# Whole-width 32x32 transposes, weight conversion on three engines, the Fourier stage beside held-back MLP tiles, and chunk loads in one piece, in a DeltaNet + Fourier-mix + MLP kernel

## The chip, the core and the metric

One core of a Trainium2 chip runs the whole program. The metric is device time in microseconds (us) of one execution, lower is better. [...] Each engine executes its own instructions strictly in the order in which they stand, and waits on semaphores for the others.

## The reference

Two blocks, joined by a reshape. `B, H, S, D = 4, 8, 768, 48`, so `DM = H*D = 384`, and the MLP is 384 -> 1536 -> 384.

```python
def _attn_ref(q, k, v, beta):
    k_n = k / (np.linalg.norm(k, axis=-1, keepdims=True) + 1e-06)
    state = zeros((B, H, D, D))
    for t in range(S):
        y[:, :, t] = einsum('bhd,bhde->bhe', q[:, :, t], state)
        v_old = einsum('bhde,bhd->bhe', state, k_n[:, :, t])
        state = state + beta_t * einsum('bhd,bhe->bhde', k_n[:, :, t], v[:, :, t] - v_old)
    return y

def _moe_ref(x, w_ch1, w_ch2):                # x = y as (B, S, DM)
    u = x + real(fft(fft(x, axis=1), axis=2))
    un = (u - mean(u)) / sqrt(var(u) + 1e-06)  # over the last axis
    return u + maximum(un @ w_ch1, 0) @ w_ch2
```

The MLP weights arrive as 64-bit floats, seen by the kernel as pairs of 32-bit words, and are turned into 32-bit floats on the chip.

## The kernel before, in words

**Attention, in chunks of 64 time steps.** A *step* `m` of the main loop is one chunk of one batch (12 chunks a batch, 48 steps). `chain(m)` does it for all 8 heads: `pk` (matmul with the state), `R` (DVE), `pu` (matmul with `wt`, the inverse of a 64x64 triangular matrix per chunk and head), `U` (ACT), `pS` and the new state `st` (DVE), then the output `py`, which ACT writes into `x`. The next step needs the new state.

**Preparation.** Four chunks of a batch are a *quad* `Q` (12 of them), two quads a *group* `g` (6 of them, 8 steps each). `prepare(Q)` loads k and q, normalises k (`Ksq`, `nrm`, `kp`), transposes both on PE (`pt`, `KQT`), makes the products `pg`, and masks them: DVE multiplies `pg` by `bm` (mask times beta, made on POOL) into `A`, and by the causal mask into `LQ`. `invert(g)` inverts the triangular matrices of a group: four DVE transposes of 32 partitions each (`X<-A`), 30 pairs of `sub`/`X` instructions of DVE that invert the 32x32 diagonal blocks, six more transposes (`wt<-X`, `T1<-X`), two rounds of small matmuls `pj` with ACT copies between them (`js`, `wt`) for the off-diagonal blocks, and a POOL multiplication of `wt` by beta. `ahead(g)` is the two `prepare` and the `invert` of a group, and runs as a generator (`pre`) during the eight steps of the group before.

**After a batch.** `post(b)` is the side generator (`side`) during the steps of the next batch: the Fourier stage (sums and differences of `x` into `scr`, matmuls `pf` and `pb`, eight DVE additions of each `pb` into `x`, the row statistics), then the MLP in three groups of 256 rows (`un`, `ptr`, `unT`; 12 tiles `ph`, each turned to `hT` by ACT and DVE in turn; `po`; the addition into `x`; the store). During batch 0 the side generator is `weights()`: six pieces of 1.5 MB land in the buffer that `hT` also uses, and each is converted in three parts of 512 columns, by ten DVE instructions and one POOL multiplication. After the last step, `post(3)` runs alone.

**Order.** In the main loop each step yields three times; between the yields the loop advances `pre` and `side` by fixed shares (6 and 8 a step). From the emitted program a scheduler makes each engine's instruction order; on the chip that order is fixed. The k, q and v chunks are loaded by SP, one DMA of 64 rows and four heads each (three DMAs at the middle of a sequence, where a row is skipped); k lands in `K4`, q in the only `qp` buffer.

Of the kernel before, what the change touches and what calls it, by code (L numbers as in the profile page):

```python
# [80 lines left out]
def kernel(  # L81
# [63 lines left out]
    def chunk_at(n):  # L145


        lo = n < NCH // 2
        return n * CH + (1 if lo else 0), CH - 1 if n == NCH // 2 - 1 else CH

    def fetch(Q, *pairs):
# [1 line left out]
        for dst, src in pairs:
            for hh in range(2):
                hs = slice(4 * hh, 4 * hh + 4)
                for c in range(QT):
                    t0, m = chunk_at(QT * i + c)
                    cuts = (0, m) if m == CH else (0, 48, m)
                    for a, z in zip(cuts, cuts[1:]):
                        nc.sync.dma_start(  # L160
                            out=dst[64 * hh + a:64 * hh + z, c, :, 0:D],
                            in_=src[b, hs, t0 + a:t0 + z, :].rearrange("h p d -> p h d"))
                    if m < CH:
                        pad = cn["zrow"].ap()[:, 0:4 * D].rearrange("p (h d) -> p h d", h=4) \
                            if src is q else src[b, hs, 0:1, :].rearrange("h p d -> p h d")
                        nc.sync.dma_start(out=dst[64 * hh + m:64 * hh + CH, c, :, 0:D], in_=pad)
# [538 lines left out]
```

## Time and profile before

| what | value |
|---|---|
| median of 3 runs (lowest, highest) | 1003.54 us (1000.3, 1005.47) |
| the profiled execution | 1004.53 us, of which its span is 1002.8 us |
| mean granted PE clock over the span | 0.81 of full speed |
| busy: PE, DVE, POOL, ACT | 748.7, 547.6, 172.4, 150.5 us |
| HBM read, written | 24.90 MB, 4.72 MB |

Read the table as shares of 1002.8 us: no engine is busy all the time, and PE, the busiest, is at 75%. The span has six stages: preparation of group 0, the steps of batches 0, 1, 2 and 3, and what follows the last step. Group 0's preparation ends where the first `R` is made (119.7 us); batches 1, 2 and 3 begin where their first state `st` is copied (269.5, 477.2 and 691.7 us), and the last step's output is in `x` at 870.8 us.

### The profile page before, as it was taken

To read this page: it belongs to the slowest core of one execution; us is meant where nothing else is said; L and a number is where in the kernel's file an instruction comes from. 1 tells how busy PE (TensorE), PEld (TensorE's weight loads), DVE (VectorE), ACT (ScalarE), POOL (GpSimd) and SP (SyncE) were. 2 spreads that over 40 slices of the span, in tenths; PEclk is the share of its full clock that TensorE was granted. 3 is DMA by queue.
4 is the path that set the end of the run, shared out by engine and by line. 5 is a ranking of instruction groups with operands and counts; after the bars stand their busy time and mean duration, and the time that the engine had idled before them with its cause. 6 is when DMAs were issued, how large, how long until landed. Compare 5 with 4: busy or idle time off the path is not lost.

```text
span 1002.8 us, 18113 instructions
## 1 busy us (share of the span) xinstructions
PE 748.7 (75%) x7768; PEld 566.9 (57%) x7768; DVE 547.6 (55%) x1200; ACT 150.5 (15%) x337; POOL 172.4 (17%) x136
## 2 busy tenths in 40 slices
PE   3400585308876979996739999898679999669998
PEld 3200474207665657764628776766566867557765
DVE  4289859887788922126793139825787111361110
ACT  1100211002120021110203120132111211110110
POOL 5323212223321040020202030031000100110000
PEclk9555556555586989997557999999879999879999
DMA  5341032222110010110200110111001000000000
GB/s 108 55 103 63 4 90 56 57 78 75 26 26 0 17 41 9 27 38 21 36 1 10 31 35 8 30 29 32 2 1 33 2 16 9 9 0 8 8 16 17
DMA packets 84360, 30.79 MB, mean 31 GB/s; under 512 B 79800, under 2 KB 81528, under 8 KB 83896
## 3 DMA queue, kind: packets, MB, share of 16 engines
q1 hardware_dynamic: 82600, 25.97, 11.6%
q0 software_dynamic: 768, 2.36, 0.6%
q8 instruction: 61, 1.00, 0.4%
q10 hardware_dynamic: 912, 1.31, 0.4%
q14 instruction: 19, 0.16, 0.1%
HBM read 24.90 MB, written 4.72 MB: 30 GB/s over the span
## 4 chain that ended last, share of the span: by engine, by line
PE 51%; DVE 30%; POOL 5%; SPq 5%; issue 4%; DMA 2%; ACT 2%; POOLq 0%; DVEq 0%; ACTq 0%
PE ph L124 17%; PE po L124 14%; PE py L124 5%; DVE X L371 5%; SPq L160 4%; DVE sub L377 3%; DVE X L379 3%; DVE wt L386 3%; DVE x L554 3%; PE pf L124 3%; PE pu L124 3%; PE pj L124 2%; PE pg L124 2%; POOL nrm L310 2%; DVE T L389 2%
## 5 line engine op out<-in xcount | busy, mean ns | idle before, releaser
L124 PE MATMUL ph<-unT,w 128*128 128x256 f32 x864 | 208.3, 396 | 5.8 <-DVE hT L613 4.0
L124 PE MATMUL po<-w,hT 128*128 128x384 f32 x576 | 192.5, 489 | 0.0
L124 PEld LDWEIGHTS ph<-unT,w 128*128 128x128 f32 x864 | 164.9, 196 | 32.1 <-DVE hT L613 4.9
L124 PEld LDWEIGHTS po<-w,hT 128*128 128x128 f32 x576 | 107.6, 190 | 70.2 <-issue 0.3
L613 DVE TENSOR_SCALAR hT<-ph 128x256 f32<-128x256 f32 x72 | 30.4, 422 | 119.7 <-PE ph L124 119.4
L623 DVE TENSOR_TENSOR x<-x,po 128x384 f32<-128x384 f32 x24 | 13.3, 554 | 130.5 <-PE po L124 130.4
L124 PE MATMUL pj<-wt,A 32*32 32x32 f32 x768 | 19.7, 214 | 81.1 <-DVE wt L386 81.1
L499 POOL DMA_INDIRECT out_dram<-x,rows_hi x12 | 12.7, 1060 | 333.0 <-DVE x L623 165.3
L127 PE MATMUL pt<-pack,kp 128*128 128x128 f32 x96 | 26.7, 374 | 52.1 <-DVE kp L313 51.2
L124 PEld LDWEIGHTS pj<-wt,A 32*32 32x32 f32 x768 | 17.8, 129 | 84.4 <-issue 61.4
L379 DVE TENSOR_TENSOR X<-X,sub 128x30 f32<-128x30 f32 (+9 forms) x180 | 62.7, 348 | 3.3
L377 DVE TENSOR_TENSOR sub<-X 128x30 f32<-128x30 f32 (+9 forms) x180 | 61.6, 342 | 2.9
L124 PE MATMUL py<-st,KQT 128*64 128x96 f32 x384 | 50.4, 284 | 5.7 <-DVE LQ L357 5.7
L611 ACT ACTIVATE hT<-ph 128x256 f32<-128x256 f32 x72 | 27.7, 384 | 165.3 <-PE ph L124 158.4
L124 PE MATMUL pu<-R,wt 64*64 64x48 f32 x768 | 39.1, 251 | 14.8 <-DVE R L452 14.8
L124 PE MATMUL pk<-st,KQT 48*64 48x48 f32 x768 | 30.6, 256 | 25.8 <-DVE st L472 9.9
L124 PEld LDWEIGHTS pu<-R,wt 64*64 64x64 f32 x768 | 33.8, 164 | 26.7 <-POOL wt L415 9.2
L472 DVE TENSOR_TENSOR st<-st,pS 48x192 f32<-48x192 f32 x88 | 30.9, 351 | 31.9 <-PE pS L124 30.3
L288 POOL TENSOR_TENSOR w<-wtmp 128x512 f32<-128x512 f32 x18 | 26.4, 1468 | 117.7 <-DVE wtmp L287 117.7
L386 DVE STREAM_TRANSPOSE wt<-X 32x1024 f32<-32x1024 f32 x24 | 46.3, 1930 | 0.6
L371 DVE STREAM_TRANSPOSE X<-A 32x1024 f32<-32x1024 f32 x24 | 45.7, 1902 | 0.2
L124 PEld LDWEIGHTS py<-st,KQT 128*64 128x64 f32 x384 | 40.0, 159 | 10.2 <-issue 4.3
(98 smaller groups left out, 1007.8 us busy)
## 6 DMA issues: line engine op xcount, KB each, us to landing
w<-in_moe_w_ch_dram SPq DMA_DIRECT2D x6, 1536.0 KB
K<-in_k_dram SPq DMA_DIRECT2D x88, 48.0 KB
qp<-in_q_dram SPq DMA_DIRECT2D x88, 48.0 KB
V<-in_v_dram SPq DMA_DIRECT2D x88, 48.0 KB
out_dram<-x SPq DMA_DIRECT2D x8, 192.0 KB
out_dram<-x SPq DMA_DIRECT2D x4, 168.0 KB
stab<-k_stab ACTq DMA_DIRECT2D x1, 640.5 KB
dtab<-k_dtab ACTq DMA_DIRECT2D x1, 384.0 KB
```

What stands on the lines that cost most here:

```text
L124: nc.tensor.matmul(o, lhsT=lhsT, rhs=rhs, start=start, stop=stop, skip_group_check=True)
L127: nc.tensor.matmul(o, lhsT=src, rhs=ident[0:src.shape[0], 0:src.shape[0]], is_transpose=True, start=start, stop=True, skip_group_check=True)
L160: nc.sync.dma_start(out=dst[64 * hh + a:64 * hh + z, c, :, 0:D], in_=src[b, hs, t0 + a:t0 + z, :].rearrange("h p d -> p h d"))
L288: nc.gpsimd.tensor_tensor(dst.rearrange("p c f -> p (c f)")[:, cs], man.bitcast(F32), exp.bitcast(F32), op=ALU.mult)
L371: nc.vector.transpose(X[pr], A[pr, :, :, c0:c0 + W].rearrange("p c u s -> p s (c u)"))
L377: nc.vector.tensor_tensor(t, X[:, j:j + 1, j + 1:].broadcast_to([128, j, n]), X[:, 0:j, j:j + 1].broadcast_to([128, j, n]), op=ALU.mult)
L379: nc.vector.tensor_tensor(X[:, 0:j, j + 1:], X[:, 0:j, j + 1:], t, op=ALU.add)
L386: nc.vector.transpose(wt[pr, :, :, c0:c0 + W].rearrange("p c u t -> p t (c u)"), X[pr].rearrange("p s t -> p t s"))
L472: nc.vector.tensor_tensor(nst[pr, :, :, e, :], st[pr, :, :, e, :], pS[pr], op=ALU.add)
L554: nc.vector.tensor_tensor(dst, dst, src, op=op)
L611: nc.scalar.activation(hT[:, fc, :], ph, ACT.Relu)
L613: nc.vector.tensor_scalar(hT[:, fc, :], ph, 0.0, None, op0=ALU.max)
```

## The change

Five things are changed, all in one diff.

1. `invert` transposes 128 partitions in one DVE instruction, three times a group in place of ten times 32 partitions. `A` now holds the unscaled diagonal and off-diagonal blocks, which ACT copies out of `pg` (six copies of 32 partitions for two chunks) in place of DVE's multiplication by `bm`; beta comes in after the transpose (`X = -X * beta`, DVE) and before the second one (`Y`, a POOL `affine_select` and a DVE multiplication). The POOL multiplications for `bm` and `wt` go, four more ACT copies a quad fill `wt`.
2. `weights` converts four parts of 384 columns a piece: two instructions on ACT, three on DVE, three on POOL a part.
3. A load is one DMA of 64 rows everywhere; k lands in one of four `kp` buffers and is normalised in place, q in one of two `qp` buffers, and loads are issued as soon as a buffer is free. The first two quads' q are issued by ACT, and the first v after the loads of k.
4. `post` is split: `second(b)` runs the third MLP group of batch b-1 beside the Fourier stage of batch b (`both`: a turn each), then the first two MLP groups of batch b. After the last step there are four MLP groups and a Fourier stage, before it three and one. `hT` is made by ACT alone, and the next group's `un`, `ptr`, `unT` stand before `po`.
5. `pre` and `side` are advanced by fractions a yield: 2.4, and 1.2, 2.0, 2.4, 2.4 for batches 0 to 3.

```diff
-    kps = [zeroed([128, QT, 4, 64], f"kp{i}", nc.gpsimd if i else nc.vector) for i in range(NB)]
-    qps = [zeroed([128, QT, 4, 64], f"qp{i}", nc.vector) for i in range(1)]
+    kps = [zeroed([128, QT, 4, 64], f"kp{i}", nc.gpsimd if i else nc.vector) for i in range(NB + 1)]
+    qps = [zeroed([128, QT, 4, 64], f"qp{i}", nc.vector) for i in range(2)]
...
+    def loads():
+        while at["load"] < min(len(quads), at["chain"] + len(kps), at["prepare"] + len(qps)):
+            load(at["load"])
+            at["load"] += 1
 
     def load(Q):
-        K4 = wk.tile([128, QT, 4, D], F32, tag="K4", name="K4")
-        qp = qps[Q % len(qps)]
-        fetch(Q, (K4, k), (qp, q))
+        kp, qp = kps[Q % len(kps)], qps[Q % len(qps)]
+        fetch(Q, nc.sync, kp, k)
+        fetch(Q, nc.scalar if Q < 2 else nc.sync, qp, q)
...
+        NP = 4
         for i, (_, dst) in enumerate(pieces):
             w64 = staged(i)
...
+                tmp = wk.tile([128, 4, DFF // NP], I32, tag="F", name="wtmp")
+                a, sg, pw, low = tmp[:, 0], tmp[:, 1], tmp[:, 2], tmp[:, 3].bitcast(F32)
+                nc.scalar.activation(low, lo.bitcast(mybir.dt.uint32), ACT.Copy, scale=2.0 ** -52)
+                nc.scalar.activation(a.bitcast(F32), hi.bitcast(F32), ACT.Abs, scale=2.0 ** 16)
+                nc.gpsimd.tensor_scalar(a.bitcast(F32), a.bitcast(F32), FLOOR, None, op0=ALU.max)
+                nc.vector.tensor_scalar(sg, hi, -2 ** 31, None, op0=ALU.bitwise_and)
+                nc.vector.scalar_tensor_tensor(a, a, 3, sg, op0=ALU.logical_shift_left,
+                                               op1=ALU.bitwise_or)
+                nc.vector.tensor_scalar(pw, a, -2 ** 23, None, op0=ALU.bitwise_and)
+                yield
+                nc.gpsimd.tensor_tensor(low, low, pw.bitcast(F32), op=ALU.mult)
+                nc.gpsimd.tensor_tensor(dst.rearrange("p c f -> p (c f)")[:, cs], low,
+                                        a.bitcast(F32), op=ALU.add)
                 yield
...
-            nc.vector.tensor_tensor(ce(A[:, at:at + 2]), pv[:, :, :, 0], ce(bm), op=ALU.mult)
+            for hh in range(2):
+                for r in range(2):
+                    pr = slice(64 * hh + W * r, 64 * hh + W * r + W)
+                    for sl in range(r + 1):
+                        c0 = W * (r - sl)
+                        nc.scalar.activation(ce(A[pr, ns, :, sl]), pv[pr, :, :, 0, c0:c0 + W],
+                                             ACT.Copy)
...
-        for i in range(4):
-            pr, c0 = slice(32 * i, 32 * i + 32), W * (i % 2)
-            nc.vector.transpose(X[pr], A[pr, :, :, c0:c0 + W].rearrange("p c u s -> p s (c u)"))
+        nc.vector.transpose(X.rearrange("p s t -> p (s t)"),
+                            A[:, :, :, 0].rearrange("p c u s -> p s (c u)"))
+        yield
+        bt = blane[:, g]
+        nc.vector.scalar_tensor_tensor(X, X, -1.0, bt[:, None, :].broadcast_to([128, W, W]),
+                                       op0=ALU.mult, op1=ALU.mult)
+        Y = wk.tile([128, W, W], F32, tag="Y", name="Y")
+        nc.gpsimd.affine_select(out=Y, in_=bt[:, :, None].broadcast_to([128, W, W]),
+                                pattern=[[-1, W], [1, W]], compare_op=ALU.is_ge, fill=0.0,
+                                base=0, channel_multiplier=0)
...
+        nc.vector.tensor_tensor(Y, Y, X, op=ALU.mult)
+        yield
+        Z = wk.tile([128, 2 * QT, 4, W], F32, tag="X", name="Z")
+        nc.vector.transpose(Z.rearrange("p c u t -> p t (c u)"), Y.rearrange("p s t -> p t s"))
+        yield
+        nc.vector.transpose(A[:, :, :, 0].rearrange("p c u s -> p s (c u)"),
+                            Y.rearrange("p s t -> p (s t)"))
...
+                    if step == 0:
+                        nc.scalar.activation(A[r1, ns, :, 1], pj[r1, hh], ACT.Copy, scale=-1.0)
+                        nc.scalar.activation(wt[r1, :, :, 0:W], Z[r1, ns], ACT.Copy)
+                    else:
+                        nc.scalar.activation(wt[r1, :, :, W:], pj[r1, hh], ACT.Copy)
+                        nc.scalar.activation(wt[r2, :, :, W:], Z[r2, ns], ACT.Copy)
...
-                if fc % 2:
-                    nc.scalar.activation(hT[:, fc, :], ph, ACT.Relu)
-                else:
-                    nc.vector.tensor_scalar(hT[:, fc, :], ph, 0.0, None, op0=ALU.max)
+                nc.scalar.activation(hT[:, fc, :], ph, ACT.Relu)
...
+    def second(b):
+        if b > 0:
+            yield from both(mlp(b - 1, [TH - 1]), fourier(b))
+            xs.pop(b - 1)
+        else:
+            yield from fourier(b)
+        yield from mlp(b, list(range(TH if b == B - 1 else TH - 1)))
...
+    PRE, SIDE = 2.4, (1.2, 2.0, 2.4, 2.4)
...
+        for _ in chain(m):
+            due[0] += PRE
+            due[1] += SIDE[b]
+            while max(due) >= 1.0:
+                for i, gen in ((1, side), (0, pre)):
+                    if due[i] >= 1.0:
+                        due[i] -= 1.0
+                        advance(gen)
```

The orders of three places follow. The first is DVE at the end of group 0's inversion: the last `sub`/`X` instruction and what stands between it and the first matmuls `pj`. Before:

```order
L379 TENSOR_TENSOR X<-X,sub 128x30
L386 STREAM_TRANSPOSE wt_72<-X 32x32x32
L389 STREAM_TRANSPOSE T_462<-X 32x32x32
L386 STREAM_TRANSPOSE wt_72<-X 32x32x32 x2
L389 STREAM_TRANSPOSE T_462<-X 32x32x32
L386 STREAM_TRANSPOSE wt_72<-X 32x32x32
L269 TENSOR_SCALAR wtmp<-w_867 128x512
```

Now:

```order
L381 TENSOR_TENSOR X<-X,sub 128x30
L384 TENSOR_TENSOR Y<-Y,X 128x1024
L276 TENSOR_SCALAR wtmp<-w_891 128x384
L388 STREAM_TRANSPOSE Z<-Y 128x32x32
L390 STREAM_TRANSPOSE A<-Y 128x32x32
```

Six transposes of 32 partitions became a multiplication and two transposes of 128 partitions, with one instruction of the weights among them.

The second is a part of the weights on DVE. Before, the part that follows the rows above (ten instructions, of 512 columns):

```order
L269 TENSOR_SCALAR wtmp<-w_867 128x512
L273 TENSOR_SCALAR wtmp<-w_867 128x512
L271 TENSOR_SCALAR wtmp<-wtmp 128x512
L278 TENSOR_SCALAR wtmp<-w_867 128x512
L274 SCALAR_TENSOR_TENSOR wtmp<-wtmp 128x512
L280 TENSOR_SCALAR wtmp<-wtmp 128x512
L285 TENSOR_SCALAR wtmp<-w_867 128x512
L282 TENSOR_SCALAR wtmp<-wtmp 128x512
L283 TENSOR_SCALAR wtmp<-wtmp 128x512
L287 TENSOR_TENSOR wtmp<-wtmp 128x512
```

Now, the first two parts of the first piece, amid group 0's inversion:

```order
L276 TENSOR_SCALAR wtmp<-w_661 128x384
L379 TENSOR_TENSOR sub<-X 128x220
L381 TENSOR_TENSOR X<-X,sub 128x11x20
L379 TENSOR_TENSOR sub<-X 128x228
L277 SCALAR_TENSOR_TENSOR wtmp<-wtmp 128x384
L381 TENSOR_TENSOR X<-X,sub 128x12x19
L280 TENSOR_SCALAR wtmp<-wtmp 128x384
L379 TENSOR_TENSOR sub<-X 128x234
L381 TENSOR_TENSOR X<-X,sub 128x13x18
L379 TENSOR_TENSOR sub<-X 128x238
L276 TENSOR_SCALAR wtmp<-w_661 128x384
```

Ten instructions a part became three, with three or so of the inversion's between the first and the second and between the third and the next part's first; the part's other work stands on ACT (ahead of L277) and POOL (ahead of L277, and behind L280).

The third is PE where batch 2 begins (the two matmuls `p` make its first state). Before:

```order
L124 MATMUL pu<-R,wt_72 64x48 x8
L124 MATMUL p_3823<-v0m,k_114 48x192 x2
L124 MATMUL py<-U,LQ 64x48 x8
L127 MATMUL pt<-pack,kp_68 128x128 x2
L127 MATMUL pt<-pack,qp_70 128x128 x2
L127 MATMUL pt<-pack,kp_68 128x128 x2
L127 MATMUL pt<-pack,qp_70 128x128 x2
L124 MATMUL pf<-stab,scr 128x65
L124 MATMUL pf<-stab,scr 65x65
```

Now:

```order
L124 MATMUL p_3748<-v0m,k_126 48x192 x2
L124 MATMUL ph<-unT,w_139 128x256
L124 MATMUL py<-U,LQ 64x48 x8
L124 MATMUL ph<-unT,w_139 128x256 x2
L124 MATMUL pf<-stab,scr 128x65
L124 MATMUL ph<-unT,w_139 128x256 x2
L124 MATMUL pf<-stab,scr 128x64
L124 MATMUL ph<-unT,w_139 128x256
L124 MATMUL pf<-stab,scr 128x2x64 x4
L124 MATMUL pf<-stab,scr 65x65
```

Among the Fourier matmuls `pf` there now stand `ph` of the MLP group that was held back from batch 0; before, there was none.

## Rows read from the trace of the kernel before

**Rows 1.** The page's busy time, share of the span and instructions, by engine.

```profile
PE 748.7 (75%) x7768; PEld 566.9 (57%) x7768; DVE 547.6 (55%) x1200; ACT 150.5 (15%) x337; POOL 172.4 (17%) x136
```

**Rows 2.** Windows: start:end, length, busy PE, PEld, DVE, ACT, POOL; clock, DMA share, GB/s.

```profile
0.00:119.70 119.70, 30.74 (x500) 24.70 (x504) 79.94 (x159) 12.20 (x23) 43.33 (x33) 0.62 0.30 69
119.70:269.50 149.80, 83.19 (x1330) 70.74 (x1323) 120.23 (x254) 21.38 (x48) 40.54 (x26) 0.53 0.23 62
269.50:477.20 207.70, 177.25 (x1784) 132.41 (x1785) 110.60 (x240) 33.77 (x77) 34.20 (x26) 0.86 0.12 24
477.20:691.70 214.50, 184.95 (x2060) 137.60 (x2061) 123.26 (x269) 39.34 (x88) 34.86 (x27) 0.87 0.11 23
691.70:870.80 179.10, 159.98 (x1654) 118.55 (x1654) 82.21 (x196) 30.48 (x71) 11.95 (x13) 0.94 0.05 12
870.80:1002.80 132.00, 112.57 (x454) 82.87 (x454) 31.37 (x85) 13.30 (x30) 7.52 (x11) 0.93 0.03 9
269.50:368.60 99.10, 77.89 (x858) 59.28 (x857) 76.06 (x170) 18.04 (x39) 22.18 (x18) 0.83 0.12 24
477.20:533.40 56.20, 34.68 (x379) 27.80 (x379) 46.80 (x116) 10.27 (x21) 10.95 (x11) 0.53 0.09 16
863.30:870.80 7.50, 4.98 (x112) 4.14 (x112) 1.40 (x4) 1.83 (x5) 0.00 (x0) 1.00 0.01 3
93.00:101.00 8.00, 0.00 (x0) 0.00 (x0) 7.81 (x15) 0.00 (x0) 1.30 (x1) 0.50 0.55 197
```

**Rows 3.** The chain of waits after the last step: start us, us, what.

```profile
874.95 4.29 PE pf L124 x24
...
880.04 3.39 PE pf L124 x24
883.44 1.71 PE pb L124 x8
...
933.39 15.81 PE ph L124 x72
949.20 15.49 PE po L124 x48
...
990.04 0.57 DVE x L623
```

**Rows 4.** The timeline of group 0's preparation: start us, us, engine, line, operation.

```profile
31.39 1.47 POOL L307 TENSOR_TENSOR Ksq<-K 128x768 f32<-128x768 f32 x1 [6.93 <-DMA qp<-in_q_dram]
...
38.49 5.21 SPq L160 DMA_DIRECT2D K<-in_k_dram  x8
...
49.47 7.58 DVE L371 STREAM_TRANSPOSE X<-A 32x1024 f32<-32x1024 f32 x4
...
71.83 6.45 POOL L307 TENSOR_TENSOR Ksq<-K 128x768 f32<-128x768 f32 x1 [9.73 <-DMA K<-in_k_dram]
...
96.87 1.90 DVE L386 STREAM_TRANSPOSE wt<-X 32x1024 f32<-32x1024 f32 x1
...
108.08 0.43 DVE L269 TENSOR_SCALAR wtmp<-w 128x512 int32<-128x512 int32 x1
```

**Rows 5.** The page's groups of the inversion's DVE instructions and of the weights' POOL multiplication.

```profile
L379 DVE TENSOR_TENSOR X<-X,sub 128x30 f32<-128x30 f32 (+9 forms) x180 | 62.7, 348 | 3.3
L377 DVE TENSOR_TENSOR sub<-X 128x30 f32<-128x30 f32 (+9 forms) x180 | 61.6, 342 | 2.9
...
L288 POOL TENSOR_TENSOR w<-wtmp 128x512 f32<-128x512 f32 x18 | 26.4, 1468 | 117.7 <-DVE wtmp L287 117.7
```

**Rows 6.** Busy time of the instructions on the weights' tile `wtmp`, whole span.

```profile
0.00:1002.80 1002.80, 87.11 (x180) 26.43 (x18) 0.81 0.13 31
```

**Rows 7.** Groups by form: ACT copies, and the weights' instruction with two inputs.

```profile
L332 ACT ACTIVATE KQT<-pt 128x256 f32<-128x256 f32 x24 | 9.2, 385 | 29.3 <-PE pt L127 28.9
...
L602 ACT ACTIVATE unT<-ptr 128x384 f32<-128x384 f32 x24 | 11.3, 490 | 88.4 <-PE ptr L127 87.9
...
L274 DVE SCALAR_TENSOR_TENSOR wtmp<-wtmp 128x512 f32<-128x512 int32 x18 | 12.3, 682 | 0.0
```

More of the change, by code (lines that the diff above doesn't have):

```diff
@@ L143, with fetch @@
     loaded = {}
[L145 to L151, printed above, removed]
+    def fetch(Q, eng, dst, src):
         b, i = quads[Q]
[L153 to L166, printed above, removed]
+        for hh in range(2):
+            for c in range(QT):
+                n = QT * i + c
+                t0 = n * CH + (1 if n < NCH // 2 else 0)
+                eng.dma_start(out=dst[64 * hh:64 * hh + CH, c, :, 0:D],
+                              in_=src[b, 4 * hh:4 * hh + 4, t0:t0 + CH, :].rearrange("h p d -> p h d"))
@@ L424, in chain @@
             held.pop(Q - 1, None)
+            at["chain"] = Q
+            loads()
             if Q + 1 < len(quads):
@@ L602, in post @@
                 nc.scalar.activation(unT[:, :, 128 * tt:128 * tt + 128], pt, ACT.Copy)
-            yield
+            return unT
+        unT = transposed(groups[0])
+        yield
+        for i, g in enumerate(groups):
             hT = wk.tile([128, KF, GT * 128], F32, tag="hT", name="hT")
@@ L644, in ahead, with both @@
             yield from prepare(Q)
-            if Q + 1 < len(quads):
-                load(Q + 1)
+            at["prepare"] = Q + 1
+            loads()
         yield from invert(g)
+    def both(*gens):
+        gens = list(gens)
+        while gens:
+            gens = [gen for gen in gens if advance(gen)]
+            yield
+    def second(b):
[5 more added lines that the diff above has]
+        yield from mlp(b, list(range(TH if b == B - 1 else TH - 1)))
     STEPS = B * NCH
     NG = len(quads) // 2
+    PRE, SIDE = 2.4, (1.2, 2.0, 2.4, 2.4)
     run(ahead(0))
+    values(0)
     tables()
     side, pre = weights(), iter(())
+    due = [0.0, 0.0]
     for m in range(STEPS):
@@ L662 @@
             pre = ahead(g) if g < NG else iter(())
-        live = True
-        step = chain(m)
-        shares = [6, 8]
-        while live or any(shares):
-            live = live and advance(step)
-            for i, gen in enumerate((pre, side)):
-                for _ in range(2):
-                    if shares[i]:
-                        shares[i] -= 1
+            due = [0.0, 0.0]
+        for _ in chain(m):
[5 more added lines that the diff above has]
+                        due[i] -= 1.0
                         advance(gen)
     run(side)
-    run(post(B - 1))
+    run(second(B - 1))
 _INS = ['q', 'k', 'v', 'beta', 'moe_w_ch1', 'moe_w_ch2']
```

147 lines of the change are left out of this document (57 added, 90 removed).

## The prediction

> **What bounds the kernel now.** I read the busy shares first: PE leads, and only at 75% [rows 1]. An average over stages with different limits says little, so the next view is the busy time by stage [rows 2]. There the kernel falls in two. Up to 269.5 us it is DVE's: DVE works 80 of the first 119.7 us and 120 of the next 149.8, PE 31 and 83 at a clock near half. From 269.5 us on it is PE's, except where DVE holds PE up: in batches 1 to 3 PE is busy for 85 to 89% of the time, but in the first 99 us of batch 1 DVE is busy for 76, and in the first 56 us of batch 2 for 47, with the clock at 0.53. The chain of waits after the last step then shows what PE costs when nothing holds it: an MLP group is 15.81 us of ph and 15.49 of po, a Fourier stage two pf of 4.29 and 3.39 and three pb of 1.71 [rows 3]. The timeline of group 0 shows what DVE spends on one inversion: ten transposes of 1.9 us around 30 pairs of short instructions [rows 4], and these are 62.7 and 61.6 us over six groups, 20.7 a group [rows 5].
>
> **DVE's work, part by part.** Transposes go from ten to three a group. No row has one of 128 partitions: between the same 1.9 us as 32 partitions with as many columns, and four times that. [...] The scaling by beta and the product Y add two instructions of 1024 columns, about 1.3 us each by the weights' two-input instruction (0.68 for 512) [rows 7]; the multiplication of pg by bm leaves. The weights took 87.1 us of DVE [rows 6]; now 24 parts of three instructions, at three quarters of 0.4 to 0.7 us, are 1.2 us a part, 29 us.
>
> **What goes to ACT and POOL.** ACT gets 144 copies of 256 columns (0.385 us each), 72 hT of as many, some 48 copies for wt and 48 instructions of the weights at about 0.49 [rows 7]: 150 us become about 285, a third of the span, in gaps that PE's own work leaves; only in group 0 does nothing cover them. affine_select has no row; anything from 1 to 6.5 us hides under the 20.7 us of pairs. It costs what exceeds these.
>
> **Stage 1, group 0: 119.7 becomes 99.** Today the second quad's Ksq starts at 31.39, after a wait for loads that stood behind those of v [rows 4]. With both quads' loads in front it can start some 13 us earlier, but 24 ACT copies of 0.385 (9.2 us) now stand in the path: the transposes of X begin between 36 and 49.5 us, I take 45. One transpose and the scaling later, at 48, the pairs begin (before: 57). The first weight piece is issued behind 64 chunk loads of 0.65 us each [rows 4], with some waits for free q buffers at 49, and lands within 8 us, since the window of 8 us around one holds 197 GB/s, all of its 1.57 MB [rows 2]. DVE meets the first weight instruction at 54 and waits to 57. Four parts at 5.7 us (below) end the pairs at 81; product and two transposes end at 87 (before: 108.1). From there to the first R I keep the 11.6 us of before: a POOL multiplication goes, ACT copies come.
>
> **Stage 2, batch 0: 149.8 becomes 123.** DVE no longer bounds it, the weights' own loop does. `tmp` has one buffer, so a part must finish before the next starts: two ACT instructions (0.98), three on POOL, two of DVE (1.0). POOL takes 0.73 us for 384 columns by the free Ksq (1.47 for 768) and 1.1 by the weights' multiplication (1468 ns for 512) [rows 4, 5]; 2.6 for three. That is 4.6, plus a wait for the DVE instruction in progress (0.35) three times: 5.7. A piece is three parts, the ACT share of the fourth (1.5) and 7 for the next DMA, which the w64 buffer holds back: 25.6. Six from 49 us, 4 for the last part, and 14 for the two ends of inversions, where the order has no part to run, give 221; I take 222. Bounds: 4.6 us a part (-22) to 8 (+46). POOL and DVE also stand in each other's way: the Ksq of 71.83 took 6.45 us beside the inversion, against 1.47 [rows 4]. [...]
>
> **Stages 3 to 5.** What PE needs at full clock: 32 us an MLP group with its row transposes, 13 a Fourier stage, 2.5 a step (4.98 for two [rows 2]), 30 for twelve; and preparation, what is left of batch 3's 160 us: 21, in batches 1 and 2, with half a group more, 27. So batches 1 and 2 need 166 each today and batch 3 about 154 at full clock; they last 42, 48 and 25 us longer.
> Batch 1 now has two MLP groups: 134. Its first four steps stay DVE's, since nothing is held back yet: 76.1 of DVE less 13.3 and 1 for A and hT, 62, and 16 of the 23 us of waits: 78 in place of 99.1, with 55 of PE's work inside. With 3 more in the rest: 160 (207.7 before).
> Batch 2: 166. At its start DVE needs 46.8 less 13.3, 33, and the pj round 7, before the first R; in those 40 us PE now has 26 us to do, most of it the held-back ph, where it had next to no MLP. 12 us remain idle at the clock it then gets: 178 (214.5).
> Batch 3: its start has 76 us of PE's work (four steps, 39 us of MLP, the Fourier stage, pj and pt) over about 59 of DVE: 154 + 5 = 159 (179.1).
>
> **Stage 6: 132 becomes 155.** Four MLP groups and a Fourier stage are 141; before, 109 took 119.2 us (870.8 to 990.0 [rows 3]), and the held-back ph now fills those 10; 12.8 us from the last addition to the end stay. 141 + 1 + 12.8.
>
> **The sum.** 99 + 123 + 160 + 178 + 159 + 155 = 874, and 1.7 that the profiled execution (1004.53) has beyond its span of 1002.8: **876 us**, against 1004.5; that execution lies 1.0 above the median of 1003.5. One batch's MLP group only moves: 32 us out of batch 1, 32 into stage 6, so the gain is in idle time: about 21 and 27 from stages 1 and 2, 80 from the rest.
>
> **The rivals.**
> *The loop is slow.* POOL and DVE hold each other up, and a part takes 8 us: 922. For it: 6.45 for 1.47 us. Against: most weight multiplications beside the same pairs kept near their mean.
> *Nothing hides.* ph, pf and pb share two PSUM buffers and one order; if pb's DVE additions keep both, the held-back group fills nothing, and idle is as before: 16 + 36 + 20 + 9 more, 957. For it: eight DVE additions follow each pb. Against: PE's order has other work between.
> *Wide transposes cost four times:* 18 times 5.7 is 103 us, some 75 of it uncovered: 951. [...]
> *Slower than before:* POOL starves. 72 POOL instructions stand in the loop, which sets stage 2; 128.5 us more need 1.8 us of wait on average for each, and half of them at the 5 us of the 71.83 row give 180, so 1056. Against: DVE itself stops at L277 until POOL has delivered, so a POOL instruction waits for the two or three pairs' instructions ahead of that, about 1 us.
> *Better:* parts at 4.6, and batches 1 and 2 with no more idle time than batch 3: 876 - 22 - 22 = 832.
>
> **How the numbers follow.** Forecast 0.62; slow loop 0.13; better 0.10; nothing hides 0.07; wide transposes 0.05; starved POOL 0.03. 876 is the likeliest; 830 to 930 holds it, the slow loop and the better case, 0.85, and the loop's bounds. Half a per cent is about what a measurement of this kernel can tell: all cases but the starved POOL are faster by more, with 0.02 for mixtures that end near 1004: faster 0.95, same 0.02, slower 0.03.
>
> **What would show it.** Right: transposes of 128 partitions at 1.9 us; first R near 99; the last weight instruction near 222 and DVE waits for POOL's `wtmp` of about 1 us a part; batch 2's first 40 us with ph among pf and a clock above 0.53; about 155 us after the last step. Wrong: POOL instructions of several us; PE idle before ph in batches 2 and 3; X<-A at 7 us.

## The result and the profile after

The changed kernel takes **929.1 us** (median of 4 runs, 928.2 to 929.5) against 1001.9 for the kernel before on the same chip: a ratio of 0.927 (95% interval 0.924 to 0.930). The gain is 73 us where 128 were forecast; the time lies 0.9 us inside the stated range of 830 to 930. The profiled execution took 929.47 us, its span is 927.8.

The page's busy line, which answers to [rows 1], and the shares of the chain that ended last, by engine (in this profile PE runs the matmuls, PEld their weight loads, DVE, ACT and POOL the elementwise work, and SPq is SP's queue of DMAs):

```profile
PE 734.9 (79%) x7768; PEld 548.2 (59%) x7768; DVE 411.7 (44%) x970; ACT 278.7 (30%) x649; POOL 176.2 (19%) x160
...
PE 57%; DVE 18%; POOL 10%; ACT 6%; issue 4%; DMA 3%; SPq 2%; POOLq 0%; DVEq 0%; ACTq 0%
```

DVE lost 136 us of work, and POOL, busy for a fifth of the span, now makes 10% of the chain (5% before). The windows of the six stages answer to [rows 2] (same columns), the seventh row is the start of batch 1 (to the `R` of its fifth step), the eighth that of batch 2 (to its first `R`):

```profile
0.00:104.50 104.50, 25.49 (x492) 21.57 (x492) 62.58 (x121) 30.97 (x67) 41.79 (x40) 0.68 0.35 83
104.50:247.90 143.40, 76.67 (x1310) 65.12 (x1312) 76.83 (x169) 54.22 (x125) 68.37 (x59) 0.56 0.25 67
247.90:413.10 165.20, 149.21 (x1683) 110.37 (x1684) 86.15 (x216) 54.34 (x130) 20.41 (x17) 0.86 0.14 27
413.10:607.90 194.80, 180.38 (x2056) 132.09 (x2056) 96.67 (x228) 67.80 (x157) 28.41 (x21) 0.92 0.10 22
607.90:774.10 166.20, 161.37 (x1662) 116.36 (x1663) 64.23 (x172) 46.72 (x111) 8.91 (x11) 0.98 0.05 13
774.10:927.80 153.70, 141.79 (x571) 102.70 (x569) 25.23 (x69) 24.70 (x60) 8.35 (x12) 0.98 0.03 11
247.90:330.90 83.00, 68.13 (x824) 54.05 (x824) 61.48 (x154) 30.27 (x68) 18.21 (x15) 0.77 0.12 22
413.10:456.40 43.30, 32.67 (x420) 26.21 (x424) 32.38 (x73) 17.79 (x35) 12.76 (x9) 0.80 0.08 15
```

Stage by stage, forecast and measured: 99 and 104.5; 123 and 143.4; 160 and 165.2; 178 and 194.8; 159 and 166.2; 155 and 153.7. Stages 2 and 4 carry 37 of the 54 us that are missing. In stage 2 no engine works for more than 54% of the time, so something waits there; in stage 4 PE itself is busy for 93%.

Three more views of the changed kernel. First the groups of DVE's transposes and of the weights' instructions, and the inversion's pairs, which answer to [rows 5] (busy us, mean ns, idle time before them and what ended it):

```profile
L388 DVE STREAM_TRANSPOSE Z<-Y 128x1024 f32<-128x1024 f32 x6 | 12.3, 2042 | 0.1
L364 DVE STREAM_TRANSPOSE X<-A 128x1024 f32<-128x1024 f32 x6 | 11.6, 1932 | 4.4 <-ACT A L350 4.4
L277 DVE SCALAR_TENSOR_TENSOR wtmp<-wtmp 128x384 int32<-128x384 int32 x24 | 13.4, 557 | 22.5 <-POOL wtmp L275 22.4
L276 DVE TENSOR_SCALAR wtmp<-w 128x384 int32<-128x384 int32 x24 | 8.8, 368 | 16.6 <-POOL w L283 11.9 <-DMA w<-in_moe_w_ch_dram 4.5
...
L381 DVE TENSOR_TENSOR X<-X,sub 128x30 f32<-128x30 f32 (+9 forms) x180 | 67.9, 377 | 4.3
L379 DVE TENSOR_TENSOR sub<-X 128x30 f32<-128x30 f32 (+9 forms) x180 | 66.3, 369 | 4.7
...
L275 POOL TENSOR_SCALAR wtmp<-wtmp 128x384 f32<-128x384 f32 x24 | 29.4, 1225 | 84.4 <-ACT wtmp L274 84.4
L282 POOL TENSOR_TENSOR wtmp<-wtmp 128x384 f32<-128x384 f32 x24 | 25.4, 1059 | 31.7 <-DVE wtmp L280 31.7
L283 POOL TENSOR_TENSOR w<-wtmp 128x384 f32<-128x384 f32 x24 | 24.4, 1016 | 1.9
```

The transposes of 128 partitions last about what those of 32 did (2042 and 1932 ns for the 1.9 us of [rows 4]). The pairs got slower (369 and 377 ns for 342 and 348), and DVE stands for 34 us before its weight instructions because of POOL. The timeline of some microseconds within group 0's inversion shows how (start us, us, what; in brackets the idle time before it):

```profile
57.18 0.40 DVE L379 TENSOR_TENSOR sub<-X 128x228 f32<-128x228 f32 x1
57.21 1.41 POOL L275 TENSOR_SCALAR wtmp<-wtmp 128x384 f32<-128x384 f32 x1 [35.15 <-ACT wtmp L274]
58.65 0.56 DVE L277 SCALAR_TENSOR_TENSOR wtmp<-wtmp 128x384 int32<-128x384 int32 x1 [1.07 <-POOL wtmp L275]
59.12 0.39 DVE L381 TENSOR_TENSOR X<-X,sub 128x228 f32<-128x228 f32 x1
59.43 0.35 DVE L280 TENSOR_SCALAR wtmp<-wtmp 128x384 int32<-128x384 int32 x1
59.70 0.40 DVE L379 TENSOR_TENSOR sub<-X 128x234 f32<-128x234 f32 x1
59.87 1.08 POOL L282 TENSOR_TENSOR wtmp<-wtmp 128x384 f32<-128x384 f32 x1 [1.25 <-DVE wtmp L280]
60.13 1.07 DVE L381 TENSOR_TENSOR X<-X,sub 128x234 f32<-128x234 f32 x1
61.02 1.05 POOL L283 TENSOR_TENSOR w<-wtmp 128x384 f32<-128x384 f32 x1
61.24 1.10 DVE L379 TENSOR_TENSOR sub<-X 128x238 f32<-128x238 f32 x1
...
63.26 1.16 POOL L275 TENSOR_SCALAR wtmp<-wtmp 128x384 f32<-128x384 f32 x1 [1.19 <-ACT wtmp L274]
63.40 0.62 DVE L381 TENSOR_TENSOR X<-X,sub 128x240 f32<-128x240 f32 x1
```

At 57.6 DVE has nothing to do but wait for POOL's maximum: the next pair stands behind L277 in its queue. At 60.13 and 61.24 its pairs start beside POOL's two-input instructions and last 1.07 and 1.10 us in place of 0.39; they end about 0.25 us after POOL's. The one-input maximum costs less: the pair's instruction that starts 0.14 us after it (63.40) lasts 0.62 us and ends before it. The one at 57.18 started ahead of the maximum and kept its 0.40 us; there the maximum itself took 1.41 us in place of 1.16.

### The profile page after: what moved, and what is told of

Same layout as the page of the kernel before. It is cut to its first block, busy times and chain, and to the rows that moved or that the text cites. A ratio compares the mean times of both kernels' runs of the same rounds, so it can differ in the third digit from the quotient of the medians.

```text
span 927.8 us, 18288 instructions
## 1 busy us (share of the span) xinstructions
PE 734.9 (79%) x7768; PEld 548.2 (59%) x7768; DVE 411.7 (44%) x970; ACT 278.7 (30%) x649; POOL 176.2 (19%) x160
## 3 DMA queue, kind: packets, MB, share of 16 engines
q10 hardware_dynamic: 5408, 2.06, 0.9%
## 4 chain that ended last, share of the span: by engine, by line
PE 57%; DVE 18%; POOL 10%; ACT 6%; issue 4%; DMA 3%; SPq 2%; POOLq 0%; DVEq 0%; ACTq 0%
PE po L124 19%; PE ph L124 17%; PE py L124 6%; PE pu L124 3%; POOL nrm L305 3%; PE pf L124 3%; DVE X L381 2%; DVE sub L379 2%; PE pt L127 2%; POOL wtmp L275 2%; POOL wtmp L282 2%; PE pg L124 2%; POOL w L283 2%; SPq L153 2%; ACT A L350 1%
## 5 line engine op out<-in xcount | busy, mean ns | idle before, releaser
L124 PE MATMUL ph<-unT,w 128*128 128x256 f32 x864 | 220.5, 402 | 2.0 <-ACT hT L623 0.9
L124 PE MATMUL po<-w,hT 128*128 128x384 f32 x576 | 203.0, 500 | 0.0
L124 PEld LDWEIGHTS ph<-unT,w 128*128 128x128 f32 x864 | 162.7, 197 | 28.5 <-issue 2.5
L623 ACT ACTIVATE hT<-ph 128x256 f32<-128x256 f32 x144 | 55.3, 384 | 189.3 <-PE ph L124 188.8
L124 PE MATMUL pj<-Z,A 32*32 32x32 f32 x768 | 18.3, 212 | 79.8 <-DVE Z L388 79.8
L475 DVE TENSOR_TENSOR st<-st,pS 48x192 f32<-48x192 f32 x88 | 30.8, 350 | 89.6 <-PE pS L124 88.4
L636 DVE TENSOR_TENSOR x<-x,po 128x384 f32<-128x384 f32 x24 | 13.3, 552 | 118.2 <-PE po L124 118.2
L124 PEld LDWEIGHTS pj<-Z,A 32*32 32x32 f32 x768 | 16.9, 127 | 81.4 <-DVE Z L388 47.6
L455 DVE TENSOR_TENSOR R<-V,pk 128x192 f32<-128x192 f32 x48 | 16.9, 352 | 96.7 <-PE pk L124 96.3
L350 ACT ACTIVATE A<-pg 32x256 f32<-32x256 f32 x144 | 48.9, 370 | 23.5 <-PE pg L124 21.4
L464 ACT ACTIVATE U<-pu 128x192 f32<-128x192 f32 x48 | 15.9, 331 | 113.6 <-PE pu L124 113.4
L488 ACT ACTIVATE x<-py 64x384 f32<-64x384 f32 x44 | 21.3, 484 | 81.9 <-PE py L124 81.7
L275 POOL TENSOR_SCALAR wtmp<-wtmp 128x384 f32<-128x384 f32 x24 | 29.4, 1225 | 84.4 <-ACT wtmp L274 84.4
```

The costliest lines, as they stand in the source:

```text
L124: nc.tensor.matmul(o, lhsT=lhsT, rhs=rhs, start=start, stop=stop, skip_group_check=True)
L275: nc.gpsimd.tensor_scalar(a.bitcast(F32), a.bitcast(F32), FLOOR, None, op0=ALU.max)
L350: nc.scalar.activation(ce(A[pr, ns, :, sl]), pv[pr, :, :, 0, c0:c0 + W], ACT.Copy)
L475: nc.vector.tensor_tensor(nst[pr, :, :, e, :], st[pr, :, :, e, :], pS[pr], op=ALU.add)
L488: nc.scalar.activation(xs[b][yr, T].rearrange("p (h u d) -> p h u d", h=2, u=4), py[yr], ACT.Copy, scale=live[yr] if n == NCH // 2 - 1 els ...
L623: nc.scalar.activation(hT[:, fc, :], ph, ACT.Relu)
```

## The experiments

All twelve runs, and the changed kernel, are measured against the kernel before on the same chip; where two runs were not on one chip, their ratios are compared. The table gives the six stages of each profile, read as above (start of the first `R`, of the first `st` copy of batches 1 to 3, of the last output copy into `x`).

| run | median us | ratio to before (95%) | stages 1 to 6, us |
|---|---|---|---|
| changed kernel | 929.1 | 0.927 (0.924 to 0.930) | 104.5, 143, 165, 195, 166, 154 |
| two_tmp | 935.7 | 0.932 (0.929 to 0.936) | 114, 147, 160, 195, 166, 154 |
| two_w64 | 928.2 | 0.926 (0.924 to 0.929) | 111, 143, 160, 195, 164, 153 |
| piped_weights | 934.9 | 0.933 (0.929 to 0.937) | 132.5, 129, 159, 195, 164, 153 |
| no_conversion | 878.6 | 0.875 (0.871 to 0.878) | 89, 121, 160, 197, 165, 153 |
| or_low_words | 908.9 | 0.909 (0.905 to 0.912) | 103, 130, 159, 195, 164, 153 |
| dve_weights | 910.8 | 0.911 (0.907 to 0.915) | 105.5, 128, 162, 195, 164, 153 |
| narrow_transposes | 997.9 | 0.996 (0.994 to 0.998) | 122, 150, 178, 217, 176, 154 |
| no_held_tile | 942.7 | 0.941 (0.938 to 0.944) | 105, 144, 202, 189, 166, 136 |
| idle_pool_pairs | 930.2 | 0.924 (0.922 to 0.927) | 112, 145, 158, 197, 165, 153 |
| old_loads_and_hT | 928.1 | 0.924 (0.922 to 0.925) | 104, 136, 168, 196, 165, 156 |
| held_weights | 899.0 | 0.893 (0.891 to 0.896) | 89, 135, 160.5, 197, 165, 153 |
| held_weights_pre4 | 905.6 | 0.900 (0.897 to 0.903) | 90.5, 131, 159, 207, 164, 153 |

**Is it the loop of the weights?** The prediction's theory (A): single buffers make a serial loop, and its length is stage 2.

```diff
-                tmp = wk.tile([128, 4, DFF // NP], I32, tag="F", name="wtmp")
+                tmp = wk.tile([128, 4, DFF // NP], I32, tag=("F", "scr")[part % 2], name="wtmp")
```

> The parts of the weights alternate between two scratch buffers (`F` and `scr`, which nothing else uses in batch 0), so that ACT may begin a part before POOL has ended the one before. Theory A, the weights' serial loop sets stage 2: a part takes POOL's three instructions and one change of engine, about 4.5 us, in place of the 5.5 to 6.2 read in the trace; some 18 parts that are not held back by a DMA gain 1 us each, so stage 2 falls from 143 to about 125 and the time from 929 to some 911. Theory B, the attention path (preparation, inversion, pj, steps) sets it and the weights only ride along: no change, 926 to 931.

```diff
+        w64s = wk.tile([128, 2, half, 2], I32, tag="hT", name="w64")
...
-            t = wk.tile([128, DFF, 2], I32, tag="hT", name="w64")
+            t, src = w64s[:, i % 2], pieces[i][0]
```

> The staging buffer of the weights is filled in two halves, so that one half is loaded while the other is converted; the scratch buffer stays single. Theory A: the 10 to 12.6 us between the last part of a piece and the first of the next become the 5.7 us of any part, five times, about 25 us, of which the gaps at the ends of inversions keep some: time about 910. Theory B: 926 to 931.

In the third kernel the first four instructions of a part are issued a round ahead (`front`):

```diff
+            if k + 1 < NP * len(pieces):
+                nxt = front(k + 1)
+            yield
+            nc.vector.scalar_tensor_tensor(a, a, 3, sg, op0=ALU.logical_shift_left,
```

> Both at once, and the order turned: ACT's two instructions, POOL's maximum and DVE's sign of part k+1 are issued a round before DVE's and POOL's rest of part k, so that neither stands in its queue for the other. Theory A: the loop falls to POOL's 3.3 us a part and hides behind the rest; stage 2 falls to its next limit, DVE's and PE's 77 us of work with the inversions' ends, about 110, and the time to some 895. Theory B: 924 to 931.

The fourth leaves the conversion out:

```diff
+                nc.scalar.activation(dst.rearrange("p c f -> p (c f)")[:, cs], hi.bitcast(F32), ACT.Copy)
                 yield
                 yield
```

> Leaves out the conversion of the weights: one ACT copy of the high words stands for the eight instructions of a part, so the MLP works with wrong weights; loads and pacing stay. It measures what the conversion costs in all, in whichever form. Theory A: stage 2 falls to 100 to 110 us, the time to 885 to 896, and two_tmp, two_w64 and piped_weights get a part of it. Theory B: DVE is 32 us freer but still waits for the same chain: 915 to 925.

Measured: 935.7, 928.2, 934.9 and 878.6. Theory A falls: piped_weights has its last part done at 173 us, not 253, and stages 1 and 2 end later than before, at 261 for 248. The faster loop only put more parts into group 0's inversion, and stage 1 grew (114, 111, 132.5). Theory B, that the weights ride along at no cost, falls by no_conversion: 38 us of stages 1 and 2 are the conversion's, 16 of them in stage 1; stage 2 still takes 121 us, above the 100 to 110 that theory A gave. (Its profiled execution took 886.9 us, 8 more than its median, so the gain in its stages is, if anything, understated.) What a part costs is seen in the inversion. The two groups of pairs of group 0 alone, of the changed kernel:

```profile
L381 DVE TENSOR_TENSOR X<-X,sub 128x30 f32<-128x30 f32 (+14 forms) x30 | 13.2, 439 | 0.8
L379 DVE TENSOR_TENSOR sub<-X 128x30 f32<-128x30 f32 (+14 forms) x30 | 13.1, 437 | 0.8
L277 DVE SCALAR_TENSOR_TENSOR wtmp<-wtmp 128x384 int32<-128x384 int32 x4 | 2.2, 558 | 2.4 <-POOL wtmp L275 2.4
...
L276 DVE TENSOR_SCALAR wtmp<-w 128x384 int32<-128x384 int32 x4 | 1.4, 351 | 4.5 <-DMA w<-in_moe_w_ch_dram 4.5
```

and of no_conversion:

```profile
L363 DVE TENSOR_TENSOR sub<-X 128x30 f32<-128x30 f32 (+14 forms) x30 | 10.0, 332 | 1.0
L365 DVE TENSOR_TENSOR X<-X,sub 128x30 f32<-128x30 f32 (+14 forms) x30 | 9.9, 332 | 1.0
```

From the scaling of `X` to the product `Y` the inversion lasts 39.5 us with four parts in it and 23.3 without: 16.2 us, made of 5.0 of DVE's own weight instructions, 6.4 by which the pairs are longer (26.3 for 19.9), 4.5 of waiting for the first DMA and 2.4 for POOL's maximum, less some overlap.

**Which part of the conversion?** New theories: C, POOL's two-input instructions hold DVE up; D, only DVE's own instructions count.

```diff
-                nc.vector.tensor_scalar(pw, a, -2 ** 23, None, op0=ALU.bitwise_and)
                 yield
-                nc.gpsimd.tensor_tensor(low, low, pw.bitcast(F32), op=ALU.mult)
-                nc.gpsimd.tensor_tensor(dst.rearrange("p c f -> p (c f)")[:, cs], low,
-                                        a.bitcast(F32), op=ALU.add)
+                nc.vector.scalar_tensor_tensor(dst.rearrange("p c f -> p (c f)")[:, cs].bitcast(I32),
+                                               lo, 29, a, op0=ALU.logical_shift_right,
+                                               op1=ALU.bitwise_or)
```

> POOL's multiplication and addition and ACT's conversion of the low words go; DVE puts the three bits of the low word in with one more two-input instruction (the weights are truncated where they were rounded). Per part DVE keeps three instructions (0.35, 0.56, 0.56 us), POOL one with a single input. Theory C, DVE is held up by POOL's two-input instructions: in the trace of the changed kernel a short DVE instruction beside one lasts about 1.0 us in place of 0.35, and 29 were hit, 19 us on the path; with these gone and one change of engine less a part the time falls to about 905. Theory D, only DVE's own instructions for the weights count (32 us before, 35 now): 926 to 934.

The next one takes `weights` from the kernel before, three parts of 512 columns a piece:

```diff
-                nc.gpsimd.tensor_scalar(a.bitcast(F32), a.bitcast(F32), FLOOR, None, op0=ALU.max)
...
+                nc.vector.tensor_scalar(man, hi, 3, 0x007FFFF8, op0=ALU.logical_shift_left,
+                                        op1=ALU.bitwise_and)
...
-    PRE, SIDE = 2.4, (1.2, 2.0, 2.4, 2.4)
+    PRE, SIDE = 2.4, (2.4, 2.0, 2.4, 2.4)
```

> The weights are converted as in the kernel before: 18 parts of ten DVE instructions (87 us of DVE) and one POOL multiplication; the side work of batch 0 is paced at 2.4 in place of 1.2, since its rounds are 90 in place of 48. Theory C and D, DVE's instructions for the weights stand on the path of stages 1 and 2: 55 us more of DVE, less some stalls beside POOL: 960 to 985. Theory A, a loop that hides behind the path unless it is the longest: a part in DVE alone needs 4.8 us, 87 in all over 200 us, so the loop would no longer bind: 900 to 925.

Measured: 908.9 and 910.8. Theory D falls twice: or_low_words has more of DVE's own work for the weights than the changed kernel (its three groups of weight instructions are 36.5 us for 31.9) and is some 18 us faster by the ratios; and the conversion on DVE alone, 82.5 us of it, costs stages 1 and 2 only 23.5 us over no_conversion, where the three engines' cost 38. I expected 960 to 985 there by both theories, so this was a miss of mine too, and that the time lies in the range that theory A gave (900 to 925) does not bring A back after piped_weights. **With the conversion put back to DVE, and the pacing that goes with it, the changed kernel is 16 to 18 us faster: the second part of the change costs that much.** By these runs DVE's free time covers most of its own instructions, and less of the time in which it stands still for another engine. The windows of stages 1 and 2 of dve_weights show DVE at work for 102 of 127.9 us in stage 2, where the changed kernel has 77 of 143.4:

```profile
0.00:105.50 105.50, 29.57 (x492) 24.65 (x492) 68.02 (x145) 25.04 (x55) 30.01 (x28) 1.00 0.35 82
105.50:233.40 127.90, 77.33 (x1310) 65.11 (x1312) 101.92 (x243) 37.01 (x89) 26.46 (x17) 0.68 0.28 75
```

To part contention from a shorter chain, or_low_words got the two POOL instructions back, on scratch data for which nobody waits:

```diff
+                wf = dst.rearrange("p c f -> p (c f)")[:, cs]
+                nc.gpsimd.tensor_tensor(idle[:, 0], wf, idle[:, 2], op=ALU.mult)
+                nc.gpsimd.tensor_tensor(idle[:, 1], wf, idle[:, 2], op=ALU.add)
                 yield
```

> or_low_words (908.9) with POOL's two two-input instructions put back as idle work: after each part a multiplication and an addition of 384 columns on scratch data, for whose result nobody waits. Theory C, such an instruction holds DVE up: some 30 of the 48 meet a DVE instruction of two inputs, 0.65 us each: 920 to 930, and short DVE instructions beside them last about 1.0 us. Theory E, what or_low_words gained was the shorter loop, not the missing contention: 907 to 912.

Measured 930.2, ratio 0.924 for 0.909: work for whose result nobody waits costs some 16 us by the ratios, so theory E as put, no change, falls, and theory C holds in part. The timeline of it, again in group 0's inversion:

```profile
60.60 1.01 POOL L281 TENSOR_TENSOR idle<-w,idle 128x384 f32<-128x384 f32 x1 [1.51 <-DVE w L277]
60.67 1.15 DVE L273 TENSOR_SCALAR wtmp<-w 128x384 int32<-128x384 int32 x1
61.57 1.10 POOL L282 TENSOR_TENSOR idle<-w,idle 128x384 f32<-128x384 f32 x1
61.74 1.19 DVE L377 TENSOR_TENSOR sub<-X 128x234 f32<-128x234 f32 x1
62.64 1.31 POOL L272 TENSOR_SCALAR wtmp<-wtmp 128x384 f32<-128x384 f32 x1
62.97 0.58 DVE L379 TENSOR_TENSOR X<-X,sub 128x234 f32<-128x234 f32 x1
63.99 0.56 DVE L274 SCALAR_TENSOR_TENSOR wtmp<-wtmp 128x384 int32<-128x384 int32 x1 [0.44 <-POOL wtmp L272]
```

Idle work costs in two ways: DVE's instructions beside it last 1.15 and 1.19 us, and the maximum, for which DVE waits, queues behind it. The pairs of the whole span rise from 121.3 us in or_low_words to 132.8 (the changed kernel: 134.2), and DVE's waits for the maximum between 40 and 250 us from 16.3 to 28.5. The two are of like size, so by estimate only about half of the price is the contention that theory C named; the other half is POOL's queue, which also lengthens a part (maxima in group 0's inversion start 4.9 us apart, in or_low_words 3.3). No run has the one without the other.

**The other parts of the change, undone one by one.** Narrow transposes, for each of the three:

```diff
-        nc.vector.transpose(X.rearrange("p s t -> p (s t)"),
-                            A[:, :, :, 0].rearrange("p c u s -> p s (c u)"))
+        for i in range(4):
+            pr = slice(32 * i, 32 * i + 32)
+            nc.vector.transpose(X[pr].rearrange("p s t -> p (s t)"),
+                                A[pr, :, :, 0].rearrange("p c u s -> p s (c u)"))
```

> Each of the three transposes of a group on 128 partitions becomes four on 32 partitions with as many columns; the rest stays. By the rows a narrow one lasts the same 1.9 us: 54 more, 103 us of DVE, of which those in groups 0, 1 and 2, 17 us each, and the starts of batches 2 and 3 in part are uncovered: 985 to 1005. If a narrow one cost a quarter of a wide one: 929.

Measured 997.9, as expected: 69 us, in all stages with an inversion (18, 6, 12, 22 and 10 us by the table). Its row for the first of the three, 24 in place of 6:

```profile
L366 DVE STREAM_TRANSPOSE X<-A 32x1024 f32<-32x1024 f32 x24 | 46.0, 1917 | 12.8 <-ACT A L350 12.4
```

This is nearly as much as the change as a whole brings, but the kernel before had ten narrow ones a group and this run has twelve: in proportion (42 of the 54) the change gains some 54 us by them, by estimate. The held-back group (its run also paces batch 1's side work at 2.4 in place of 2.0):

```diff
-        if b > 0:
-            yield from both(mlp(b - 1, [TH - 1]), fourier(b))
...
-        yield from mlp(b, list(range(TH if b == B - 1 else TH - 1)))
+        yield from fourier(b)
+        yield from mlp(b, list(range(TH)))
```

> The third MLP group of batches 0 to 2 is no longer held back: Fourier stage, then three groups, within the next batch's steps, paced at 2.4. If the held-back group fills idle time at the starts of batches 2 and 3: stage 3 takes 32 us more of PE's work, stage 4 loses cover for about 20, stage 5 for 15, the tail after the last step loses a group (32) but idles some 10 at its start: about 970. If nothing hides behind it, as in the rival of that name: 925 to 935.

Measured 942.7: the hold is worth 13.6 us, between the two expectations. Stage 3 takes 37 us more without it, but stage 6 is 18 shorter and stage 4 is 6 shorter, not 20 longer. Stages 3 and 4 without it, read as above:

```profile
248.90:450.80 201.90, 177.50 (x1884) 130.66 (x1884) 111.72 (x265) 65.81 (x153) 33.49 (x25) 0.91 0.13 25
450.80:639.40 188.60, 178.50 (x2003) 131.97 (x2003) 76.15 (x187) 62.51 (x148) 17.41 (x16) 0.94 0.11 23
```

PE idles 24.4 us in stage 3 without the hold and 16.0 with it, but 10.1 and 14.4 in stage 4. The held-back `ph` does fill batch 2's start, but without the hold there is little to fill: the last transpose of that batch's inversion then ends at 433.4, ahead of the batch, and the first `R` stands 11.3 us after the batch's begin; with the hold it ends at 439.2, 26 us into the batch, and `R` stands 43.3 us after its begin. So the gain of the hold is in stages 3 and 6. Stage 4, which takes 217 us with the hold and narrow transposes, is short because of the wide ones. The loads and hT (the run also puts all chunk loads on SP's queue, those of v ahead of the second quad's):

```diff
-    qps = [zeroed([128, QT, 4, 64], f"qp{i}", nc.vector) for i in range(2)]
+    qps = [zeroed([128, QT, 4, 64], f"qp{i}", nc.vector) for i in range(1)]
...
+                if fc % 2:
+                    nc.scalar.activation(hT[:, fc, :], ph, ACT.Relu)
+                else:
+                    nc.vector.tensor_scalar(hT[:, fc, :], ph, 0.0, None, op0=ALU.max)
```

> The changed kernel with two of its parts undone, which are read in different stages: one q buffer in place of two, all chunk loads on SyncE's queue and those of v ahead of the second quad's (stages 1 and 2), and hT alternating between DVE and ACT as before (stages 3 to 6). By the prediction the loads bring the second quad some 13 us earlier, so stage 1 rises from 104.5 to about 112 to 117; hT on DVE costs DVE 0.34 us each where ACT paid 0.49, and PE's need stays, so stages 3 to 6 move by less than 5 us in all: about 940. Rival, the loads hide behind the weights: 929.

Measured 928.1: no difference in all, where 940 was expected (the 0.34 and 0.49 us are not hT's: in the kernel before it took 422 ns on DVE and 384 on ACT, means of 72). With the old loads `X` is scaled 5 us later (49.0 for 43.8), yet the first `R` stands at 103.9 for 104.5; stage 2 is 7 us shorter, stages 3 to 6 together 5 us longer. Why stage 2 gains was not taken apart, and the run undoes two things at once. The new pacing, ACT's copies and the order before `po` were not undone alone, and what the parts are worth need not add up to the 73 us.

**A better version.** Group 0's inversion was kept free of weights, the low words put in as in or_low_words:

```diff
+        nc.scalar.activation(w64s[:, :, 0, :].bitcast(F32), wts[0][:, 0, 0:2, 0:2], ACT.Copy)
         w64d = {0: staged(0), 1: staged(1)}
```

> or_low_words with the first load of the weights held until group 0's inversion is over (a small ACT write into the staging buffer that reads wt), the staging buffer in two halves and two scratch buffers. No weights then stand among the pairs of the first inversion. Theory F, a part costs most inside an inversion, where DVE is the path, and little beside steps: stage 1 falls from 103 to about 89, stage 2 rises by less than that: 895 to 903. Theory G, the parts only move, and cost the same in the second inversion: 906 to 912.

> held_weights with the preparation and inversion of the next group paced at 4 rounds in place of 2.4. The X of the next group waits for the second quad, whose preparation can't start before step 4 frees its buffers; faster pacing puts it ahead of steps 5 to 7. If that is the path of stage 2 and of the first four steps of batch 1, each gains some 5 us: 8 to 12 below held_weights. If DVE's work bounds these stretches: within 3 us of held_weights.

(The second differs by `PRE`, 4.0 for 2.4.) Measured 899.0 and 905.6. Theory F holds: stage 1 falls by 14 us and stage 2 rises by 5. held_weights is 3.6% faster than the changed kernel (0.893 to 0.927) and has no wait for weights in group 0's inversion, which lasts 23.3 us again. Faster pacing was to bring 8 to 12 us and costs 7: it gains 4 in stage 2, about as expected, but only 2 in stage 3, and loses 10 in stage 4.

## Why the prediction came out as it did

**Transposes: right.** The 13.3 us a group that the sum takes off DVE are seven transposes at 1.9 us, and stand for wide ones that last no longer than narrow ones; no row of the kernel before showed that. The runs do: one of 128 partitions lasts 1.9 to 2.04 us on average, one of 32 in narrow_transposes 1.9 to 1.99; undoing the width costs 69 us, against the 75 uncovered of the rival.

**Stage 2, the step that failed: "DVE no longer bounds it, the weights' own loop does".** It forecast 123 us and the stage took 143.4. The cycle of a part was right (5.5 to 6.4 us where nothing else held it, 5.7 taken). The loop still ended at 253 and not at 222, since it stood for 20.7 and 20.5 us at the ends of the two inversions, where 14 were taken for both. But the claim that it sets the stage was wrong: with a faster loop stages 1 and 2 got longer together, and in piped_weights the loop was done at 173 and stage 2 at 261. Without the conversion, but with the weights' loads and one ACT copy a part, stage 2 takes 121 us: that much is the attention's path, and each part put on it pays for DVE's wait for POOL and for the longer pairs. The forecast did weigh contention, but asked only what a POOL instruction waits for, and "starved POOL" is refuted: POOL's slowest multiplication of the weights took 2.04 us. The price came on the other side: in the changed kernel 20 of the pairs' instructions that started beside POOL's 48 multiplications and additions of the weights lasted 0.69 to 1.10 us each and were held for some 13 us in all, by estimate, and DVE waited 34 us for POOL's results.

**Stage 1: 5.5 us late.** The pairs end at 83 (81 forecast) and the last transpose at 88.4 (87). From there to the first `R` the 11.6 us of before were kept; it took 16, since the next quads' preparation stands ahead of that `R` in DVE's order and waits twice for POOL. DVE's timeline there:

```profile
95.47 1.43 DVE L306 TENSOR_SCALAR nrm<-nrm 128x16 f32<-128x16 f32 x1 [2.53 <-POOL nrm L305]
...
97.22 0.96 DVE L308 TENSOR_TENSOR kp<-kp,nrm 128x768 f32<-128x768 f32 x1
...
102.06 1.23 DVE L306 TENSOR_SCALAR nrm<-nrm 128x16 f32<-128x16 f32 x1 [3.02 <-POOL nrm L305]
...
104.48 0.35 DVE L455 TENSOR_TENSOR R<-V,pk 128x192 f32<-128x192 f32 x1
```

The 13 us by which earlier loads were to help moved `X` by 5 and the first `R` by nothing (old_loads_and_hT).

**Stage 6: right**, 153.7 for 155, with PE busy for 141.8 us of the 141 taken. **Stage 3: right in time only**, 165.2 for 160: two errors nearly cancel. PE was busy for 149.2 us, not 134, and idled 16, not 26; its first four steps took 83 us, not 78, but with 68 us of PE's work inside, not 55, at a clock of 0.77.

**Stages 4 and 5: the idle time was right, PE's need was not.** Stage 4 idles 14.4 us (12 forecast), but PE is busy for 180.4 us, not 166; stage 5 idles 4.8 (5), with 161.4 for 154. The units were meant at full clock, and the granted clock was 0.92 in stage 4 (0.80 in its first 43 us): 180.4 times 0.92 is 166, so by this estimate the clock makes most of the difference there. It does not in stage 5: 161.4 times 0.98 is 158, where 154 were taken, although the forecast's own row had PE busy for 160 us in that stage [rows 2]. How much is the clock's was not tested; no run held it fixed. Batch 2's start went as forecast (43.3 us to the first `R` for 40, with 32.7 of PE's work inside for 26), but that the held-back group makes stage 4 shorter was wrong: without it the stage takes 188.6 us (no_held_tile).

**The rivals.** The slow loop (922) came nearest in time: POOL and DVE do stand in each other's way (a pair's instruction took 1.07 us in place of 0.39), but the parts did not last 8 us. "Nothing hides" wanted 16, 36, 20 and 9 us more in stages 3 to 6; it is refuted by their times, though in stage 4 the hold gains nothing. "Better" was not reached, four times as costly transposes are refuted by their rows. Stages 1 to 5 all took longer than forecast, 55 us in all, and that the sum stops 0.9 us short of the range's end is luck: the range reached so far to hold the slow loop at 922, and that did not come.

## What to carry to other kernels

Before work is moved from a loaded engine to two others, count what the loaded engine will wait for: where each engine takes its instructions in order, a chain that crosses engines three times a part can cost the path more than all of its instructions on one engine (38 us against 23.5 here, with 32 us of DVE's own work against 82.5). Ask of a stage first whose path sets it, by leaving the suspect out once; only then speed up a loop. And width pays where an instruction's time does not depend on its partitions, as that of the transposes here (1932 ns for 128, 1917 for 32): three for twelve were worth some 69 us, where the whole change, with ten before, is worth 73.
